# Sigmoid attention and a bilinear feed-forward in one kernel: x in seven blocks of 512 tokens through memory, and twelve float32 pairs

## The chip, the core and the metric

The kernel runs on one NeuronCore of a Trainium2 chip. The metric is the time of one execution in microseconds (us) on the device. A run's profile comes from one execution of its own; its times are not averages.

## The reference

```python
# q, k, v: 8 batches, 12 heads, 448 tokens, 64 wide; float32
scores = q @ k.T / 8 - log(448)
attn   = 1 / (1 + exp(-scores))          # a sigmoid, no row sums
x      = (attn @ v), heads side by side  # 3584 tokens x 768
h      = ((x @ w1) * (x @ w2)) @ w3      # 1024 wide, then 1024 wide
out    = h @ w_out                       # 3584 x 768
```

w1, w2, w3 and w_out come as the words of 64-bit floats, and the kernel makes float32 of them itself.

## The kernel before

**Two kinds of product.** Most products run in a reduced float32 (F32R in the code), with each operand split into a high and a low part: hi x hi, hi x lo and lo x hi are summed, three products in the place of one. `split` makes the two parts: a copy that rounds (ScalarE, VectorE) and a subtraction (VectorE or GpSimd). The alternative is a product in full float32 on unsplit operands. `PLAIN` says how many of the first head pairs do their attention that way; it is 9.

**Stages.** Heads go in pairs: 48 pairs, six to a batch (`pairs`, line 341). A pair has four chunks of keys, taken in the order 0, 3, 1, 2 (line 410); one chunk of one pair is a slot, 192 in all. In a slot TensorE makes the scores of its chunk, ScalarE the sigmoids, and one slot later TensorE multiplies with v (`attend_due`). After the last chunk `combine` (line 260) brings the pair's 128 rows of x into SBUF as two tiles xh and xl of 448 columns, one of the six pieces of 128 rows (kc) that a batch's x has. Two pools, px0 and px1, hold x of even and odd batches.

**Up products.** `up` (line 310) multiplies a batch's x with w1 and w2. For each of eight chunks of 128 features (fc) and each of the two weights (n) it sums 6 pieces x 3 products of 448 columns, so 288 products a batch; then ScalarE copies the first sum and VectorE multiplies the two into g, which is stored in memory (`g_dram`). `up` is a generator: the loop takes 12 products a slot from it (line 435), which stand between a slot's scores and the product with v of the slot before. A batch's products start in slot 2 of the batch behind it (line 432); the last batch's come after attention (line 460), beside the decode of w_out.

**Weights.** A piece of w1 or w2 is a job: load the words (768 KB), take magnitudes on ScalarE (line 79), decode in six VectorE operations (lines 86 to 102), and split three slots later (copy on ScalarE, subtraction on VectorE, line 67). `starts` (line 354) puts eight of the 16 jobs into batch 0, one in three slots, and eight into batch 1, one in 4/3 slots. The 16 pieces of w3 follow from batch 2 on, one in two pairs, loaded two slots ahead of their decode, and are stored in memory at once (line 304).

**Order.** Up to slot 34 (line 417) the order on TensorE, SP, ScalarE and GpSimd is the program's own, and VectorE's is set by a planner; after it, TensorE and SP keep the program's order. All loads and stores are issued on SP, in order. At slot 34 the pool of the weight words (`pp`) closes and the pool of the split attention operands (`pf`) takes its memory. For a split pair VectorE makes qs and kh (lines 158, 159, 66) and GpSimd kl and ks (lines 67, 165), two slots ahead of the pair where the kinds change over.

**Behind.** When the up products are done, w3 x w_out is formed (line 508) and the last product (line 524) goes over all tokens in blocks of 512, with g loaded back from memory.

Of the kernel before, what the change touches and what calls it, by code (L numbers as in the profile page):

```python
# [25 lines left out]
def sigmoid_attention_bilinear_ffn(  # L26
# [42 lines left out]
    def load_words(src, pool=None):  # L69
        if pool is None:  # L70
            raw = pd.tile([P, NK, P, 2], U32, name="raw", bufs=1)[:, :src.shape[1]]
# [5 lines left out]
    def magnitude(raw, early=False):  # L77
        f = (pp if early else pd).tile([P, *raw.shape[1:-1]], F32, name="f", bufs=3 if early else 2)
        nc.scalar.activation(f, raw[..., 1].bitcast(F32), AF.Abs, scale=HW_SCALE)  # L79
        return f  # L80

# [28 lines left out]
    px0 = phase_a.enter_context(tc.tile_pool(name="px0", bufs=NK, side="right"))  # L110
    pa = phase_a.enter_context(tc.tile_pool(name="pa", bufs=2, side="right"))
    px = (px0, px1)
# [69 lines left out]
    def add_halves(dst, src):  # L182

        for j in range(2):
            rows, others = slice(j * D, (j + 1) * D), slice((1 - j) * D, (2 - j) * D)
            nc.scalar.copy(out=dst[rows], in_=src[j][others])  # L186
            nc.vector.tensor_tensor(out=dst[rows], in0=src[j][rows], in1=dst[rows], op=ALU.add)  # L187
# [69 lines left out]
                    start=first and m == 0, stop=last and m == len(ops) - 1,  # L257
                )

    def combine(b, accs):  # L260
        xh = px[b % 2].tile([P, S], F32R, name="xh")
        xl = px[b % 2].tile([P, S], F32R, name="xl")
        if len(accs) == 1:
            split(xh, xl, accs[0][:, :S], nc.scalar.copy, nc.vector)
            return xh, xl
        t = pm.tile([P, S], F32, name="t", bufs=1)
        add_halves(t, [acc[:, :S] for acc in accs])
        split(xh, xl, t, nc.scalar.copy, nc.vector)
        return xh, xl

    wh, wl = {}, {}
    for n in (1, 2):
# [15 lines left out]

    def load_job(i):
        _, _, cs, src = jobs[i]  # L290
        raws[i] = load_words(src[:, cs], pp) if i < EARLY else load_words(src[:, cs])

    def decode_job(i):
        if i + 2 < EARLY:
            load_job(i + 2)
        for k in (i, i + 1):
            if k not in fs and k in raws:
                fs[k] = magnitude(raws[k], k < EARLY)
        f = decode(raws.pop(i), fs[i])
        if EARLY <= i + 1 < len(starts):  # L300
            load_job(i + 1)
# [8 lines left out]
    def up(b, xs, banks):  # L310

        for fc in range(NF):
            for n in (1, 2):
                acc = ps.tile([P, 512], F32, name="up", tag=next(banks), bufs=2)
                for kc in range(NK):
                    xh, xl = xs[kc]
                    for m, (w, x) in enumerate(((wh[n], xh), (wh[n], xl), (wl[n], xh))):
                        nc.tensor.matmul(  # L318
                            acc[:, :S], w[:, fc, kc], x,
                            start=(kc == 0 and m == 0), stop=(kc == NK - 1 and m == 2),  # L320
                        )
                        if (kc, m) != (NK - 1, 2):
                            yield
                if n == 1:
                    a_sb = pm.tile([P, S], F32, name="a_sb", bufs=1)
                    nc.scalar.copy(out=a_sb, in_=acc[:, :S])
                    yield
            g = pm.tile([P, S], F32, name="g", bufs=1)
            nc.vector.tensor_tensor(out=g, in0=acc[:, :S], in1=a_sb, op=ALU.mult)
            nc.sync.dma_start(out=g_dram[fc, :, b * S:(b + 1) * S], in_=g)  # L330
            yield

    def take(stream, n):
        for _ in range(n):
            next(stream, None)
# [6 lines left out]
    zeros = pp.tile([P, 512], F32R, name="zeros", bufs=1)  # L342
    nc.vector.memset(zeros.bitcast(F32), 0.0)

    def idle_products(n):

        acc = ps.tile([P, 512], F32, name="up", bufs=2)
# [5 lines left out]
    first = NPAIR * NC  # L353
    starts = [1 + 3 * i for i in range(8)] + [first + 1 + 4 * i // 3 for i in range(8)]
    assert len(starts) == 2 * NF
    later = [(2 * NPAIR + 2 * i) * NC + 1 for i in range(2 * NF)]
    steps = {}
    for i, s in enumerate(starts):
        steps.setdefault(s + (3 if s < first else 2), []).append((split_job, i))
    for i, s in enumerate(starts + [s + 2 for s in later]):  # L360
        steps.setdefault(s, []).append((decode_job, i))
    for i, s in enumerate(later):
        steps.setdefault(s, []).append((load_job, 2 * NF + i))

    EARLY = sum(s + 2 < PLAIN * NC - 2 for s in starts)
    qks, vvs = {}, {}
    for p in range(2):
        qks[p] = load_pair(*pairs[p])
# [4 lines left out]
    xs = {b: [] for b in range(B)}  # L373
    filler = iter(())
    waiting = []
    accs = {}
# [2 lines left out]
    def attend_due(slot):  # L379
        while waiting and waiting[0][0] <= slot:  # L380
            _, p, c, ops = waiting.pop(0)
            if c == 0:
                accs[p] = [
                    ps.tile([P, 512], F32, name="av", bufs=2) for _ in range(1 if p < PLAIN else 2)
                ]
            attend(c, ops, vs[p], accs[p])
            if c == NC - 2:
                b = pairs[p][0]
                xs[b].append(combine(b, accs.pop(p)))
                del vs[p]  # L390

    def prepare(p, i):
# [84 lines left out]
    TB = 512  # L477
    NH = NF // 2


# [16 lines left out]
    assert NT % TB == 0  # L497
    split_g(0, 0, load_g(0, 0))
    for ic in range(NF):
        w3h, w3l = w3s.pop(ic)  # L500
# [62 lines left out]
```

## Time and profile before

| what | us |
|---|---|
| three timed runs: median, lowest, highest | 1082.26, 1080.23, 1083.45 |
| the profiled execution's own time | 1081.56 |
| its span, first to last instruction | 1079.5 |
| TensorE, VectorE, ScalarE, GpSimd busy in it | 1067.9, 714.1, 563.4, 190.1 |

Busy is the time in which an engine has an instruction of the trace under way. A product's duration in the trace is longer than its share of TensorE, because products overlap; the chain of waits, in which n products in a row stand with the time from the first to the next thing behind them, gives what one takes. PE is TensorE, PEld its weight loads, DVE VectorE, ACT ScalarE, POOL GpSimd, SPq the queue that issues transfers. A line number is the kernel's line; `combine` and `decode` operations carry the helper's line.

### The profile page before, as it was taken

The numbers are of one execution on the slowest core, as the hardware profiler recorded it, in microseconds if no ns is written. First come the engines' busy times: TensorE is split into PE (matmuls) and PEld (weight loads), VectorE is DVE, ScalarE is ACT, GpSimd is POOL, SyncE is SP. The second block draws the span as 40 slices with busy tenths as digits, with TensorE's granted clock in tenths as the row PEclk, the third lists the DMA queues.
The fourth block names the chain that finished last, engine by engine and source line by source line (L and its number), as shares of the span: only waits on it lengthen the run. The fifth ranks groups of instructions, "written<-read, shape, count | busy, mean of one in ns | idle before, by whom it ended". The sixth has DMA issues, their size and how long they took to land.

```text
span 1079.5 us, 14155 instructions
## 1 busy us (share of the span) xinstructions
PE 1067.9 (99%) x5094; PEld 915.1 (85%) x5094; DVE 714.1 (66%) x1074; ACT 563.4 (52%) x789; POOL 190.1 (18%) x277
## 2 busy tenths in 40 slices
PE   8999899999999999999999999999999999999998
PEld 3256799999999999999999989999999888888886
DVE  5997978888878878888887877649862133223321
ACT  5855666776776677767767766653342011101100
POOL 0002432232233323232332224200000000000000
PEclk9999999999999999999999999999999999999999
DMA  8755434443543535344452543225471032233211
GB/s 257 231 166 146 103 95 122 124 132 104 140 118 103 141 107 135 112 131 115 116 154 79 135 122 92 68 75 180 137 243 39 20 127 93 84 127 127 88 49 49
DMA packets 100693, 129.15 MB, mean 120 GB/s; under 512 B 8016, under 2 KB 82960, under 8 KB 100624
## 3 DMA queue, kind: packets, MB, share of 16 engines
q1 hardware_dynamic: 100624, 128.25, 40.6%
q8 instruction: 40, 0.66, 0.3%
q14 instruction: 29, 0.24, 0.1%
HBM read 98.34 MB, written 29.88 MB: 119 GB/s over the span
## 4 chain that ended last, share of the span: by engine, by line
PE 94%; DVE 2%; DMA 1%; ACT 1%; issue 1%; SPq 0%; ACTq 0%
PE up L318 42%; PE up L524 21%; PE av L255 10%; PE sp L199 9%; PE up L508 6%; PE sp L196 2%; PE av L248 2%; PE sp L225 1%; DMA raw<-w 1%; DVE f L102 0%; ACT f L79 0%; DVE w L67 0%; DVE raw L99 0%; DVE f L94 0%; ACT ap L180 0%
## 5 line engine op out<-in xcount | busy, mean ns | idle before, releaser
L318 PE MATMUL up<-xh,w 128*128 128x448 f32 x1536 | 467.2, 368 | 0.0
L318 PEld LDWEIGHTS up<-xh,w 128*128 128x128 f32 x1536 | 288.8, 188 | 31.6 <-issue 5.9
L318 PE MATMUL up<-xl,w 128*128 128x448 f32 x768 | 281.2, 366 | 0.0
L524 PE MATMUL up<-w 128*128 128x512 f32 x1008 | 228.7, 389 | 0.0
L524 PEld LDWEIGHTS up<-w 128*128 128x128 f32 x1008 | 189.2, 188 | 39.2
L180 ACT ACTIVATE ah<-sp,bias 128x896 fp32r<-128x896 f32 x117 | 117.6, 1005 | 114.3 <-PE sp L199 113.5
L217 DVE TENSOR_TENSOR al<-sp,ah 128x896 fp32r<-128x896 f32 x117 | 127.5, 1090 | 50.0 <-ACT sp L180 49.0
L67 POOL TENSOR_TENSOR kl<-kk,kh 128x896 fp32r<-128x896 f32 x39 | 89.5, 2294 | 402.5 <-DVE kh L66 380.3
L318 PEld LDWEIGHTS up<-xl,w 128*128 128x128 f32 x768 | 144.4, 188 | 12.5
L534 DVE COPY o_sb<-up 128x512 f32<-128x512 f32 x42 | 29.0, 691 | 161.0 <-PE up L524 161.0
L66 ACT CAST w<-graw 128x1024 fp32r<-128x1024 f32 x28 | 29.4, 1056 | 175.9 <-PE up L524 170.5
L180 ACT ACTIVATE sp<-sp,bias 128x896 f32<-128x896 f32 x117 | 113.6, 971 | 0.0
L255 PE MATMUL av<-ah,vs 128*128 128x448 f32 x312 | 102.4, 368 | 3.8 <-DVE ah L239 2.7
L255 PE MATMUL av<-al,vs 128*128 128x448 f32 x234 | 86.1, 368 | 0.4 <-DVE al L217 0.4
L199 PE MATMUL sp<-qs,kh 128*128 128x448 f32 x234 | 86.3, 369 | 0.0
L67 POOL TENSOR_TENSOR vs<-vv,vs 128x256 fp32r<-128x256 f32 x78 | 68.2, 885 | 102.8 <-DVE vs L66 95.0
L199 PE MATMUL sp<-qs,kl 128*128 128x448 f32 x234 | 86.3, 369 | 0.0
L239 DVE TENSOR_TENSOR ah<-st,ah 64x448 fp32r<-64x448 f32 x78 | 59.3, 760 | 18.7 <-ACT st L180 16.8
L255 PEld LDWEIGHTS av<-ah,vs 128*128 128x128 f32 x312 | 58.5, 188 | 10.3 <-DVE ah L239 2.8
L79 ACT ACTIVATE f<-raw 128x768 f32<-128x768 f32 (+2 forms) x48 | 34.4, 716 | 48.3 <-DMA raw<-w_out 17.7
L186 ACT COPY t<-av 64x448 f32<-64x448 f32 x78 | 41.3, 529 | 32.3 <-PE av L255 31.2
L180 ACT ACTIVATE ah<-st,bias 64x448 fp32r<-64x448 f32 x78 | 52.2, 670 | 4.0 <-DVE st L187 2.0
(57 smaller groups left out, 1243.4 us busy)
## 6 DMA issues: line engine op xcount, KB each, us to landing
qq<-qT SPq DMA_DIRECT2D x78, 224.0 KB, 3.9
kk<-kT SPq DMA_DIRECT2D x78, 224.0 KB, 4.5
g_dram<-g SPq DMA_DIRECT2D x64, 224.0 KB, 2.0
graw<-g_dram SPq DMA_DIRECT2D x14, 1024.0 KB, 5.3
raw<-w SPq DMA_DIRECT2D x16, 768.0 KB, 5.3
out<-o_sb SPq DMA_DIRECT2D x42, 256.0 KB, 2.0
vv<-vL SPq DMA_DIRECT2D x48, 192.0 KB, 2.8
raw<-w3T SPq DMA_DIRECT2D x16, 512.0 KB, 4.1
```

The source lines that it names most:

```text
L66: hi_engine(out=dst_hi, in_=src)
L67: lo_engine.tensor_tensor(out=dst_lo, in0=src, in1=dst_hi, op=ALU.subtract)
L79: nc.scalar.activation(f, raw[..., 1].bitcast(F32), AF.Abs, scale=HW_SCALE)
L180: nc.scalar.activation(dst, src, AF.Sigmoid, bias=bias[:n], scale=scale)
L186: nc.scalar.copy(out=dst[rows], in_=src[j][others])
L199: nc.tensor.matmul(sp[:, j], k[:, j, at:at + n], qs[:, j], start=m == 0, stop=m == 1)
L217: nc.vector.tensor_tensor(out=al, in0=sp, in1=ah, op=ALU.subtract)
L239: nc.vector.tensor_tensor(out=a[others, j], in0=t[rows], in1=a[rows, j], op=ALU.subtract)
L255: nc.tensor.matmul(accs[j][:, :S], v[:, c, j].rearrange("p u d -> p (u d)"), a[:, j], start=first and m == 0, stop=last and m == len(ops) - 1,
L318: nc.tensor.matmul(acc[:, :S], w[:, fc, kc], x, start=(kc == 0 and m == 0), stop=(kc == NK - 1 and m == 2),)
L508: nc.tensor.matmul(acc[:, :NM], a[:, jc], w[:, jc, ms], start=(jc == 0 and m == 0), stop=(jc == NF - 1 and m == 2),)
L524: nc.tensor.matmul(acc[:, :TB], w[:, fc, ms], g[:, at, fc % NH], start=(fc == 0 and m == 0), stop=(fc == NF - 1 and m == 2),)
```

## The change

x is now kept in seven blocks of 512 tokens (the batches are of 448). The first block stays in SBUF, in six of eight tiles of 2 x 512 columns (high and low part); all of x behind its first 512 tokens is split into `xs`, stored in memory (`x_dram`) two slots later, and loaded by blocks. The up products of block c run in the slots of batches c + 2 and on, from slot 49 for block 0 and from slot 76 for block 1; before slot 76 eleven are taken a slot, then twelve. Each is of 512 columns, and there are 7 x 288 = 2016 of them, 2304 before. Block 6 comes after attention, behind the 48 products that block 5 has left there. Two tiles of the next block are loaded as chunk 6 of the eight feature chunks begins; in chunk 7 the passes of w1 and w2 are interleaved (1: pieces 0 to 3, 2: 0, 1: 4, 2: 1, 1: 5, 2: 2 to 5), and after each of the first four passes of w2 that frees a tile the next tile is asked for. g is stored after the next chunk's first sum has been copied, instead of at once.

Twelve pairs are in full float32, so the kinds change over at slot 46, and all 16 pieces of w1 and w2 are decoded before it, one in 2.7 slots, loaded three jobs ahead. A piece of w3 is loaded in the slot in which its decode stands, and stored five slots later.

```diff
-    PLAIN = 9
+    TB = 512
+    PLAIN = 2 * NPAIR
+    x_dram = dram.tile([NK, P, 2, NT], F32, name="x_dram")
-    px1 = phase_x.enter_context(tc.tile_pool(name="px1", bufs=NK, side="left"))
-    pm = phase_x.enter_context(tc.tile_pool(name="pm", bufs=2, side="left"))
+    px = phase_x.enter_context(tc.tile_pool(name="px", bufs=NK + 2, side="left"))
+    pm = phase_x.enter_context(tc.tile_pool(name="pm", bufs=1, side="left"))
-    pp = phase_p.enter_context(tc.tile_pool(name="pp", bufs=3, side="right"))
+    pp = phase_p.enter_context(tc.tile_pool(name="pp", bufs=4, side="right"))
...
+    def combine(b, kc, accs, due):
         if len(accs) == 1:
+            src = accs[0][:, :S]
+        else:
+            src = pa.tile([P, S], F32, name="t", bufs=1)
+            add_halves(src, [acc[:, :S] for acc in accs])
+        at = b * S
+        n = min(max(TB - at, 0), S)
+        if n:
+            if b == 0:
+                blocks[0][kc] = px.tile([P, 2, TB], F32R, name="x")
+            x = blocks[0][kc][:, :, at:at + n]
+            split(x[:, 0], x[:, 1], src[:, :n], nc.scalar.copy, nc.vector)
+        if n < S:
+            x = pa.tile([P, 2, S], F32R, name="xs")[:, :, n:]
+            split(x[:, 0], x[:, 1], src[:, n:], nc.scalar.copy, nc.vector)
+            stores.append((due, x_dram[kc, :, :, at + n:at + S], x.bitcast(F32), (kc, at + S)))
+
+    def store_due(slot):
+        for entry in [e for e in stores if e[0] <= slot]:
...
+            nc.sync.dma_start(out=entry[1], in_=entry[2])
+
+    def load_block(c, kc):
+        blocks[c][kc] = px.tile([P, 2, TB], F32R, name="x")
+        nc.sync.dma_start(
+            out=blocks[c][kc].bitcast(F32), in_=x_dram[kc, :, :, c * TB:(c + 1) * TB]
+        )
...
     def decode_job(i):
-        if i + 2 < EARLY:
-            load_job(i + 2)
+        if i + 3 < EARLY:
+            load_job(i + 3)
+        elif i >= EARLY:
+            load_job(i)
...
         if n == 3:
-            nc.sync.dma_start(out=w3_dram[at, :, cs], in_=f)
+            stores.append((starts[i] + 5, w3_dram[at, :, cs], f, None))
...
+    def up(c, banks):
+        xs, following = blocks[c], c + 1 if c + 1 in blocks else None
...
         for fc in range(NF):
+            if fc == NF - 2 and following:
+                for kc in range(2):
+                    load_block(following, kc)
+            passes = [(1, kc) for kc in range(NK)] + [(2, kc) for kc in range(NK)]
+            if fc == NF - 1:
+                passes.sort(key=lambda s: s[1] + 3.5 * s[0])
+            accs = {}
+            for n, kc in passes:
+                if kc == 0:
+                    accs[n] = ps.tile([P, TB], F32, name="up", tag=next(banks), bufs=2)
+                for m, (w, i) in enumerate(((wh[n], 0), (wh[n], 1), (wl[n], 0))):
+                    nc.tensor.matmul(
+                        accs[n], w[:, fc, kc], xs[kc][:, i],
+                        start=(kc == 0 and m == 0), stop=(kc == NK - 1 and m == 2),
+                    )
                     yield
+                if (fc, n) == (NF - 1, 2) and following and kc + 2 < NK:
+                    load_block(following, kc + 2)
+                if (n, kc) == (1, NK - 1):
+                    a_sb = pm.tile([P, TB], F32, name="a_sb")
+                    nc.scalar.copy(out=a_sb, in_=accs[1])
+                    if ready:
+                        store(*ready)
+            g = pm.tile([P, TB], F32, name="g")
+            nc.vector.tensor_tensor(out=g, in0=accs[2], in1=a_sb, op=ALU.mult)
+            ready = fc, g
+        store(*ready)
...
-    starts = [1 + 3 * i for i in range(8)] + [first + 1 + 4 * i // 3 for i in range(8)]
-    later = [(2 * NPAIR + 2 * i) * NC + 1 for i in range(2 * NF)]
+    EARLY = 2 * NF
+    starts = [1 + 27 * i // 10 for i in range(EARLY)]
+    starts += [(2 * NPAIR + 2 * i) * NC + 1 for i in range(2 * NF)]
+    steps = {s + 3: [(split_job, i)] for i, s in enumerate(starts[:EARLY])}
     for i, s in enumerate(starts):
         steps.setdefault(s, []).append((decode_job, i))
...
+            store_due(slot)
             prepare(p, i)
...
-            if b > 0 and (hp, i) == (0, 2):
+            if b > 1 and (hp, i) == ((0, 1) if b == 2 else (1, 0)):
                 take(filler, 10 ** 6)
-                filler = up(b - 1, xs[b - 1], itertools.repeat("up"))
-            take(filler, ups)
+                filler = up(b - 2, itertools.repeat("up"))
+            take(filler, ups if slot >= (3 * NPAIR + 1) * NC else ups - 1)
...
     attend_due(slot)
+    store_due(10 ** 6)
     take(filler, 10 ** 6)
...
-    filler = up(B - 1, xs[B - 1], banks)
+    filler = up(NT // TB - 1, banks)
```

## Rows read from the trace of the kernel before

**Rows 1.** The page's busy shares: busy us (share of span) xinstructions of each engine.
```profile
PE 1067.9 (99%) x5094; PEld 915.1 (85%) x5094; DVE 714.1 (66%) x1074; ACT 563.4 (52%) x789; POOL 190.1 (18%) x277
```
**Rows 2.** The page's chain that ended last, share of the span by line.
```profile
PE up L318 42%; PE up L524 21%; PE av L255 10%; PE sp L199 9%; PE up L508 6%; PE sp L196 2%; PE av L248 2%; PE sp L225 1%; DMA raw<-w 1%; DVE f L102 0%; ACT f L79 0%; DVE w L67 0%; DVE raw L99 0%; DVE f L94 0%; ACT ap L180 0%
```
**Rows 3.** Busy us in windows: PE, PEld, DVE, ACT, POOL, clock, DMA share, GB/s.
```profile
0.00:14.00 14.00, 12.23 (x42) 6.21 (x42) 2.61 (x6) 5.19 (x7) 0.20 (x4) 1.00 0.85 259
14.00:58.00 44.00, 42.09 (x182) 10.81 (x184) 43.17 (x60) 36.37 (x45) 0.00 (x0) 1.00 0.77 232
...
157.00:300.00 143.00, 143.00 (x702) 131.42 (x701) 117.73 (x180) 103.33 (x149) 43.47 (x65) 1.00 0.45 120
```
**Rows 4.** The chain of waits in order of time: start us, us, what xcount.
```profile
57.60 0.95 PE sp L196 x4
58.55 2.66 PE up L318 x12
61.21 0.90 PE av L248 x4
...
90.04 1.44 PE up L318 x6
...
122.88 1.49 PE sp L199 x4
...
155.19 0.81 PE sp L199 x4
...
171.54 2.44 PE up L318 x12
...
256.90 2.46 PE up L318 x12
...
714.79 2.02 PE av L255 x10
716.81 63.30 PE up L318 x312
780.12 67.08 PE up L508 x384
847.19 228.54 PE up L524 x1008
```
**Rows 5.** Timeline of VectorE in batch 0: start us, us, engine, line, operation.
```profile
20.40 0.95 DVE L67 TENSOR_TENSOR w<-f,w 128x768 fp32r<-128x768 f32 x1
...
32.20 0.95 DVE L67 TENSOR_TENSOR w<-f,w 128x768 fp32r<-128x768 f32 x1
...
36.61 0.62 DVE L67 TENSOR_TENSOR xl<-av,xh 128x448 fp32r<-128x448 f32 x1
37.14 0.95 DVE L102 TENSOR_TENSOR f<-f,raw 128x768 f32<-128x768 f32 x1
38.01 0.95 DVE L67 TENSOR_TENSOR w<-f,w 128x768 fp32r<-128x768 f32 x1
```
**Rows 6.** Groups by line: operation xcount, busy us, mean ns, idle before and releaser.
```profile
L159 DVE TENSOR_TENSOR qs<-qq,qs 64x896 fp32r<-64x896 f32 x39 | 44.7, 1146 | 1.3
...
L158 DVE CAST qs<-qq 128x896 fp32r<-128x896 f32 x39 | 24.5, 629 | 12.6 <-DMA qq<-qT 12.4
L66 DVE CAST kh<-kk 128x896 fp32r<-128x896 f32 x39 | 24.3, 622 | 0.4
...
L67 POOL TENSOR_TENSOR kl<-kk,kh 128x896 fp32r<-128x896 f32 x39 | 89.5, 2294 | 402.5 <-DVE kh L66 380.3 <-PE up L318 14.9 <-PE sp L199 7.3
```
**Rows 7.** Transfers by issuing line: xcount, KB each, median us to landing.
```profile
graw<-g_dram SPq DMA_DIRECT2D x14, 1024.0 KB, 5.3
...
raw<-w3T SPq DMA_DIRECT2D x16, 512.0 KB, 4.1
```
**Rows 8.** Who waited for whom: us in total, times, longest us.
```profile
ACT f L79 <- DMA raw<-w3T: 5.4, 5, 2.7
...
PE av L255 <- DVE t L187: 1.0, 1, 1.0
```

More of the change, by code (lines that the diff above doesn't have):

```diff
@@ L55, in sigmoid_attention_bilinear_ffn @@
     scale = 1.0 / math.sqrt(D)
-    PLAIN = 9
+    TB = 512
+    assert NT % TB == 0 and S <= TB <= 2 * S
+    PLAIN = 2 * NPAIR
     pw = ctx.enter_context(tc.tile_pool(name="pw", bufs=4))
@@ L67, in split, with load_words @@
         lo_engine.tensor_tensor(out=dst_lo, in0=src, in1=dst_hi, op=ALU.subtract)
-    def load_words(src, pool=None):
-        if pool is None:
-            raw = pd.tile([P, NK, P, 2], U32, name="raw", bufs=1)[:, :src.shape[1]]
+    def load_words(src, pool):
+        if pool is pd:
+            raw = pd.tile([P, NF // 2, P, 2], U32, name="raw", bufs=1)
         else:
@@ L75, in load_words, with magnitude @@
         return raw
-    def magnitude(raw, early=False):
-        f = (pp if early else pd).tile([P, *raw.shape[1:-1]], F32, name="f", bufs=3 if early else 2)
+    def magnitude(raw, pool=pd):
+        f = pool.tile([P, *raw.shape[1:-1]], F32, name="f", bufs=3 if pool is not pd else 2)
         nc.scalar.activation(f, raw[..., 1].bitcast(F32), AF.Abs, scale=HW_SCALE)
@@ L106, in sigmoid_attention_bilinear_ffn @@
     phase_x = ExitStack()
-    px1 = phase_x.enter_context(tc.tile_pool(name="px1", bufs=NK, side="left"))
-    pm = phase_x.enter_context(tc.tile_pool(name="pm", bufs=2, side="left"))
+    px = phase_x.enter_context(tc.tile_pool(name="px", bufs=NK + 2, side="left"))
+    pm = phase_x.enter_context(tc.tile_pool(name="pm", bufs=1, side="left"))
     phase_a = ExitStack()
-    px0 = phase_a.enter_context(tc.tile_pool(name="px0", bufs=NK, side="right"))
     pa = phase_a.enter_context(tc.tile_pool(name="pa", bufs=2, side="right"))
-    px = (px0, px1)
     phase_p = ExitStack()
-    pp = phase_p.enter_context(tc.tile_pool(name="pp", bufs=3, side="right"))
+    pp = phase_p.enter_context(tc.tile_pool(name="pp", bufs=4, side="right"))
     bias = pm.tile([P, 1], F32, name="bias", bufs=1)
@@ L258, in attend @@
                 )
-    def combine(b, accs):
-        xh = px[b % 2].tile([P, S], F32R, name="xh")
-        xl = px[b % 2].tile([P, S], F32R, name="xl")
+    blocks = {c: {} for c in range(NT // TB)}
+    stores, stored = [], {}
+    def combine(b, kc, accs, due):
         if len(accs) == 1:
[L264 to L269, printed above, removed]
+            src = accs[0][:, :S]
[15 more added lines that the diff above has]
+        for entry in [e for e in stores if e[0] <= slot]:
+            stores.remove(entry)
+            if entry[3]:
+                kc, end = entry[3]
+                stored[kc] = end
+            nc.sync.dma_start(out=entry[1], in_=entry[2])
+    def load_block(c, kc):
+        assert stored[kc] >= (c + 1) * TB
+        blocks[c][kc] = px.tile([P, 2, TB], F32R, name="x")
+        nc.sync.dma_start(
+            out=blocks[c][kc].bitcast(F32), in_=x_dram[kc, :, :, c * TB:(c + 1) * TB]
+        )
     wh, wl = {}, {}
@@ L290, in load_job @@
         _, _, cs, src = jobs[i]
-        raws[i] = load_words(src[:, cs], pp) if i < EARLY else load_words(src[:, cs])
+        raws[i] = load_words(src[:, cs], pp if i < EARLY else pd)
     def decode_job(i):
-        if i + 2 < EARLY:
-            load_job(i + 2)
+        if i + 3 < EARLY:
+            load_job(i + 3)
+        elif i >= EARLY:
+            load_job(i)
         for k in (i, i + 1):
-            if k not in fs and k in raws:
-                fs[k] = magnitude(raws[k], k < EARLY)
+            if k in raws and k not in fs:
+                fs[k] = magnitude(raws[k], pp if k < EARLY else pd)
         f = decode(raws.pop(i), fs[i])
-        if EARLY <= i + 1 < len(starts):
-            load_job(i + 1)
         n, at, cs, _ = jobs[i]
         if n == 3:
-            nc.sync.dma_start(out=w3_dram[at, :, cs], in_=f)
+            stores.append((starts[i] + 5, w3_dram[at, :, cs], f, None))
     def split_job(i):
@@ L308, in split_job, with store @@
         split(wh[n][:, at, cs], wl[n][:, at, cs], fs.pop(i), nc.scalar.copy, nc.vector)
-    def up(b, xs, banks):
-        for fc in range(NF):
[L313 to L326, printed above, removed]
-                    yield
[L328 to L331, printed above, removed]
+    def up(c, banks):
+        xs, following = blocks[c], c + 1 if c + 1 in blocks else None
+        ready = None
+        def store(fc, g):
+            nc.sync.dma_start(out=g_dram[fc, :, c * TB:(c + 1) * TB], in_=g)
+        for fc in range(NF):
+            if fc == NF - 2 and following:
[13 more added lines that the diff above has]
+                    )
+                    yield
+                if (fc, n) == (NF - 1, 2) and following and kc + 2 < NK:
[9 more added lines that the diff above has]
+        store(*ready)
@@ L341, in sigmoid_attention_bilinear_ffn @@
     pairs = [(b, hp) for b in range(B) for hp in range(NPAIR)]
-    zeros = pp.tile([P, 512], F32R, name="zeros", bufs=1)
+    zeros = pp.tile([P, TB], F32R, name="zeros", bufs=1)
     nc.vector.memset(zeros.bitcast(F32), 0.0)
     def idle_products(n):
-        acc = ps.tile([P, 512], F32, name="up", bufs=2)
+        acc = ps.tile([P, TB], F32, name="up", bufs=2)
         for _ in range(n):
@@ L351, in sigmoid_attention_bilinear_ffn @@
     idle_products(12)
-    first = NPAIR * NC
-    starts = [1 + 3 * i for i in range(8)] + [first + 1 + 4 * i // 3 for i in range(8)]
-    assert len(starts) == 2 * NF
-    later = [(2 * NPAIR + 2 * i) * NC + 1 for i in range(2 * NF)]
-    steps = {}
+    EARLY = 2 * NF
+    starts = [1 + 27 * i // 10 for i in range(EARLY)]
+    starts += [(2 * NPAIR + 2 * i) * NC + 1 for i in range(2 * NF)]
+    steps = {s + 3: [(split_job, i)] for i, s in enumerate(starts[:EARLY])}
     for i, s in enumerate(starts):
-        steps.setdefault(s + (3 if s < first else 2), []).append((split_job, i))
-    for i, s in enumerate(starts + [s + 2 for s in later]):
         steps.setdefault(s, []).append((decode_job, i))
-    for i, s in enumerate(later):
-        steps.setdefault(s, []).append((load_job, 2 * NF + i))
-    EARLY = sum(s + 2 < PLAIN * NC - 2 for s in starts)
+    assert starts[EARLY - 1] + 3 < PLAIN * NC - 2
     qks, vvs = {}, {}
@@ L372, in sigmoid_attention_bilinear_ffn @@
     splits, vs = {0: split_pair(0 < PLAIN, *qks.pop(0))}, {0: split_v(0 < PLAIN, vvs.pop(0))}
-    xs = {b: [] for b in range(B)}
+    load_job(2)
     filler = iter(())
@@ L387, in attend_due @@
             if c == NC - 2:
-                b = pairs[p][0]
-                xs[b].append(combine(b, accs.pop(p)))
+                combine(*pairs[p], accs.pop(p), slot + 2)
                 del vs[p]
@@ L475, in sigmoid_attention_bilinear_ffn @@
     p4 = ctx.enter_context(tc.tile_pool(name="p4", bufs=2, side="left"))
-    TB = 512
     NH = NF // 2
@@ L495, in split_g @@
             split(ghs[:, at, fs], gls[:, at, fs], g[:, fs], nc.scalar.copy, nc.vector)
-    assert NT % TB == 0
     split_g(0, 0, load_g(0, 0))
```

## The prediction

> **What bounds the kernel now.** I read the page's busy shares first: TensorE is busy for 99% of the span [rows 1]. A busy TensorE need not be a full one, so the chain of waits comes next: 42% of it is the up products of line 318, 21% the last product of line 524, 10% the attention products of line 255 [rows 2]. TensorE thus sets the end, and the question is what each product costs and where the engine is held up. The windows show where other engines come near: between 14 and 58 us, batch 0, VectorE is busy 43.17 of 44 us and DMA moves 232 GB/s at a share of 0.77; between 157 and 300 us the share is 0.45 [rows 3]. The chain in order of time gives the prices [rows 4]. A chunk of a float32 pair (a slot: scores 0.95, attention times v 0.90) takes 1.85 us of TensorE. Twelve up products of 448 columns take 2.44 us where x lies in one pool and 2.46 in the other, 203.3 and 205.0 ns each, and 2.66 us between float32 products. After attention 312 take 63.30 us, 202.9 each. The last product's 512 columns take 228.54/1008 = 226.7 ns, the 384 columns of line 508 67.08/384 = 174.7. The four products at 155.19 open slot 48 (pair 12); the up products end at 780.12, and the rest of the span, 299.4 us, is not touched.
>
> **The change, part by part.** I split the span at slot 48, since in the new kernel everything before it is float32 attention without up products, and everything behind it is what the old kernel does there, with 2016 up products of 512 columns instead of the 2040 of 448 that it still has at that point (2304 less the 264 of slots 26 to 47).
>
> *Behind slot 48.* The old kernel takes 780.12 - 155.19 = 624.9 us. Of that 1728 products at 204.2 and 312 at 202.9 are 352.9 + 63.3 = 416.2 us; the other 208.7 us are 36 pairs of attention and one wait of 1.0 us [rows 8], which I count below, so 207.7. In place of the 416.2 stand 2016 x 226.7 = 457.0 us, and the stretch grows to 664.7 us. The price of a 512-column product on x is not in the trace. From above it is 233.4 ns (the loop's 204.2 x 512/448: no gain by width), from below 225.4 (226.7 less the 1.3 by which places differ). I take 226.7: it is measured, on the same width and the same kind of operands. The Trainium skill (TensorE: Matmul & The Clock Gate, section Back-to-back issue gap) has a warm product cost N/2.4 + 2.5 ns, a fixed part too small for widening to pay: 2304 x 189.2 against 2016 x 215.8, 0.9 us in all. The rows differ from it at both widths, by 14 and by 11 ns, so I go by them; that width brings nothing is a rival below.
>
> *Before slot 48.* The old kernel needs 155.19 us, with 264 up products and three split pairs in it, and with a jam where the pairs change over: from 90.04 to 122.88 it gets through the rest of a float32 slot (2.66 + 0.90), two whole ones (1.85 + 2.66 each) and one split pair (15.5, a quarter of the stretch's mean of four slots: 559.6/36), 28.1 us, so 4.7 go there. The new kernel has 48 float32 slots. On TensorE alone slot 48 would come 22 x 1.85 = 40.7 us after slot 26, which begins at 57.60: at 98.3. But all 16 weight pieces of w1 and w2 are now decoded in those slots, one each 2.7 slots = 5.0 us, and VectorE needs more. Its row of the split of line 67 recurs after 5.81 us (32.20 to 38.01) with a combine of 0.53 in between, so a piece is 5.3 us [rows 5]. At 20.40 two pieces are decoded. Fourteen more are 74.2 us; eleven combines 5.8; the second part that a combine of batch 1 has (448 cut into 64 and 384) about 0.15 x 5 = 0.7. So the last decode ends at 101.1, and two splits of 0.95 end at 103.0. Only then is the memory of the weight pieces free for pair 12, whose qs and kh take 2.4 us on VectorE (0.63 + 1.15 + 0.62) and whose kl takes 2.3 on GpSimd [rows 6]: 107.7. VectorE, not TensorE, sets this stage, and the 4.7 us of the jam are not lost again, since no decode stands between these operations. Bounds: 98.3 if VectorE keeps up, 112.4 if a jam like the old one comes back. I take 107.7, from the nearest rows.
>
> Sum: 107.7 + 664.7 = 772.4 for the end of the up products against 780.1, 7.7 us less, before waits.
>
> *x through memory.* 42 stores (one a pair from the seventh on) and 36 loads are new. SP's issues hide beside TensorE, and so do the stores: x of a pair is needed only much later, except the last pair's, which has the 48 up products left after attention. What can show is the change of blocks. Six x tiles of a block and two spare ones: two tiles of the next block are loaded a chunk ahead, the others as the last chunk frees them. That chunk has twelve passes of three products; the sixth tile is asked for after the tenth pass and used in the eighteenth (the next block's sixth). Seven passes of 0.68 us lie between, 1 3/4 slots or 7.3 us inside attention (a slot is 3.9 us now, 12 x 22.5 ns more then), 4.8 us after it. A load of 512 KB lands in 4.1 us (w3 words), one of 1024 KB in 5.3 [rows 7]: alone, in time. But from the fifth pass to the eighteenth, about 12.6 us, the queue carries four loads (2.1 MB), q and k of a pair (four of 64 x 2 x 448 float32, 0.9 MB), a store of x (0.46) and one of g (0.26), 3.7 MB or 295 GB/s, and 232 GB/s at a share of 0.77 means 301 when full [rows 3]. So each of six changes lies between no wait and some 3 us (at the 259 GB/s of the first 14 us the same bytes take 1.7 us more, and landing itself varies by the 1.2 between the two rows). I take 0.4 us each, 2.5 in all, because the tiles come in the order of use and q and k have slack of slots. Queued behind a waiting product on TensorE is all else, so a wait counts in full. Behind a waiting load on SP stand the next loads of q, k and v, due slots later.
>
> *w3 pieces.* Words and decode now stand in one slot; before, the load came two slots ahead. ScalarE's abs waits for them: five of 16 waited in the old kernel, 5.4 us, 2.7 at most, and TensorE lost 1.0 once [rows 8]. Next slots have 0.27 us more of TensorE work each as cover. From below nothing, from above 16 x 1.0; I take 0.6. The late stores of g and w3 free SP, on which TensorE does not wait: nothing. g's buffer is single and its store now leaves half a chunk later, with 18 products (6 us) before its next use; if a store lands late VectorE waits: in the same allowance. Copies and products of g are 56 instead of 64, off the path.
>
> Total: -7.7 + 2.5 + 0.6 = -4.6 against the profiled execution's 1081.56 (span 1079.5 and 2.1 around it), which lies 0.7 under the median of the runs: **1077.0**.
>
> **Rivals.** *Late tiles (slower side).* At each change of blocks the last two tiles land after their pass. For: the queue's 295 GB/s against 301, and the change after attention has only 4.8 us and the w_out words beside it. Against: the share around is 0.45, and q and k wait for GpSimd, so bursts need not coincide. Price 3 us x 6 = 18: 1081.6 - 7.7 + 0.6 + 18 = 1092; the gain is gone from 1.2 us each.
> *Width brings nothing.* A 512-column product costs 233.4: 2016 x 6.7 = 13.5 us more, 1090. For: the two 448-column pools already differ. Against: line 524's 1008 products at 226.7. The gain is gone from 226.7 + 4.6/2.016 = 229.0.
> *ScalarE stands at the w3 words.* Each of 16 loads costs TensorE 1.0 us: 15.4 more than taken, 1092. For: load and use stand together. Against: eleven of 16 did not wait, and of five waits one reached TensorE.
> *TensorE sets the front.* VectorE's backlog drains under the slots: slot 48 near 99.5, 8 us less, 1069. For: batch 0's chain runs on TensorE for most of 21 to 58 us. Against: VectorE's 43.17 of 44 us at three slots a piece.
>
> **How the numbers follow.** Forecast with its small waits (1073 to 1081) 0.52; TensorE's front 0.10; late tiles, from 1 us each up to the full price, 0.18; width 0.07; w3 words 0.13. A measurement tells 0.3%, 3.2 us, from no change: below 1079.0 is faster, above 1085.5 slower. Faster: three quarters of the forecast's 0.52, all of 0.10 and 0.06 of the rest, where the waits or the width take only part of their price: 0.55. Slower: half of the three cases with waits or no width, 0.19. The rest, 0.26, is the same. Range 1068 to 1088: TensorE's front below, half of each slow rival's price above; the forecast's own is 1073 to 1081.
>
> **What would show it.** Right: up products at 226.7 ns, twelve in 2.72 us; VectorE without gaps from 14 to 103 us and slot 48's scores near 107; TensorE's waits on x loads six, under half a microsecond each. Wrong: up products above 229; the scores of slot 48 after 112; TensorE idle before up products until DMA into x for over 1 us a change; ScalarE's abs waiting over 15 us in all for the w3 words with TensorE idle behind it. The prediction fails as a whole if the sum of such waits passes 7.7 us, or slot 48 comes before 100.

## The result and the profile after

The changed kernel takes **1088.43 us** (median of six, 1086.97 to 1089.11) against 1081.8 of the kernel before: ratio 1.0062, 95% interval 1.0048 to 1.0075. The forecast was 1077.0: wrong in sign. The profiled execution takes 1087.51 us, its span 1085.7.

The page's busy shares, then the chain by line (the row in which the forecast looked for the gain):

```profile
PE 1065.1 (98%) x4818; PEld 850.3 (78%) x4818; DVE 686.2 (63%) x1030; ACT 545.9 (50%) x760; POOL 170.6 (16%) x256
...
PE up L358 40%; PE up L559 21%; PE av L256 9%; PE sp L200 8%; PE up L543 6%; PE sp L226 1%; PE av L249 1%; PE sp L197 1%; DVE w L70 1%; DVE f L97 1%; DMA raw<-w 1%; DMA qp<-kT 1%; DVE raw L102 1%; DVE f L105 1%; DMA x<-x_dram 1%
```

The up products' share fell from the 42% of [rows 2], but VectorE's lines and DMA now stand in the chain at 1% each: TensorE no longer runs through from the first slot to the last. The windows say where (us, PE, PEld, DVE, ACT, POOL busy, granted clock, DMA share, GB/s):

```profile
14.00:58.00 44.00, 39.20 (x170) 9.92 (x168) 43.28 (x62) 35.08 (x43) 0.00 (x0) 1.00 0.80 249
58.00:100.00 42.00, 35.95 (x150) 9.06 (x152) 41.24 (x61) 31.17 (x42) 0.00 (x0) 0.96 0.55 176
100.00:112.00 12.00, 10.97 (x48) 3.11 (x48) 6.62 (x9) 7.28 (x10) 4.92 (x7) 1.00 0.73 191
112.00:145.00 33.00, 30.36 (x134) 24.53 (x133) 28.31 (x38) 20.82 (x31) 9.97 (x15) 1.00 0.64 160
157.00:300.00 143.00, 142.19 (x645) 120.53 (x644) 115.01 (x172) 98.02 (x141) 42.73 (x63) 1.00 0.58 167
```

From 14 to 100 us VectorE is nearly full and TensorE lacks 11 us; between 100 and 112 neither is full; from 112 to 145, where the kinds of pair change over, TensorE lacks 2.6. From 157 on it is all but full (142.19 of 143), as in [rows 3]. The chain in order of time, inside attention and behind it:

```profile
251.96 2.75 PE up L358 x12
254.71 1.24 PE av L256 x6
255.94 0.83 PE sp L200 x4
256.77 2.75 PE up L358 x12
...
710.07 8.88 PE up L358 x39
...
724.93 61.95 PE up L358 x272
786.88 3.12 PE up L543 x18
```

Twelve products take 2.75 us where 2.72 was forecast: 229.2 ns each, and 227.8 in the row of 272 (61.95/272). The first five behind attention's 448 columns take 232.5, 235.9, 228.3, 232.5 and 230.9 from start to start, most of the rest 226.7.

Stage by stage, from the first score product of a slot. In the changed kernel those of slots 48 and 56 are these (start us, us, line, operation; in brackets the idle time before it and its releaser):

```profile
110.25 0.44 PE L200 MATMUL sp<-qs,kh 128*128 128x448 f32 x1 [0.27 <-DVE qs L160]
...
143.65 0.37 PE L200 MATMUL sp<-qs,kh 128*128 128x448 f32 x1
```

| | before | forecast | after |
|---|---|---|---|
| slot 48 begins | 155.0 | 107.7 | 110.2 |
| slot 56 begins | 186.1 | | 143.6 |
| up products end | 780.1 | 775.5 | 786.9 |
| the rest of the span | 299.4 | 299.4 | 298.8 |

The 11.4 us between forecast and trace come out as: front +2.5; slots 48 to 56 +4.4 (33.4 us, where 56 attention products at 0.207 and 77 up products at 0.227 need 29.0; I go on calling this loss the jam); up products +4.1 (0.028 at each of 143 changes of width); attention +1.1 (a pair's period, 16.77, less 48 products leaves 5.77 us, before 15.54 leaves 5.74); one loss of 1.0 at 220 us (slot 75 has only the last two up products of block 0, where its neighbours have eleven, so TensorE comes early to attention times v and stands for 0.81 us until VectorE has made `al`, the low part of the sigmoids); x tiles -1.2 (1.3 where 2.5 was forecast); w3 words -0.6. Sum 11.3.

### The profile page after: what moved, and what is told of

It reads as the page before. It is cut to its first block, busy times and chain, and to the rows that moved or that the text cites. A ratio compares the mean times of both kernels' runs of the same rounds, so it can differ in the third digit from the quotient of the medians.

```text
span 1085.7 us, 13615 instructions
## 1 busy us (share of the span) xinstructions
PE 1065.1 (98%) x4818; PEld 850.3 (78%) x4818; DVE 686.2 (63%) x1030; ACT 545.9 (50%) x760; POOL 170.6 (16%) x256
## 4 chain that ended last, share of the span: by engine, by line
PE 88%; DVE 6%; DMA 3%; ACT 1%; issue 1%; SPq 1%; POOL 0%; DVEq 0%; ACTq 0%
PE up L358 40%; PE up L559 21%; PE av L256 9%; PE sp L200 8%; PE up L543 6%; PE sp L226 1%; PE av L249 1%; PE sp L197 1%; DVE w L70 1%; DVE f L97 1%; DMA raw<-w 1%; DMA qp<-kT 1%; DVE raw L102 1%; DVE f L105 1%; DMA x<-x_dram 1%
## 5 line engine op out<-in xcount | busy, mean ns | idle before, releaser
L358 PE MATMUL up<-x,w 128*128 128x512 f32 x2016 | 485.7, 391 | 0.1
L358 PEld LDWEIGHTS up<-x,w 128*128 128x128 f32 x2016 | 378.1, 188 | 78.0 <-DMA x<-x_dram 2.0
L181 ACT ACTIVATE ah<-sp,bias 128x896 fp32r<-128x896 f32 x108 | 108.7, 1006 | 133.8 <-PE sp L200 133.7
L218 DVE TENSOR_TENSOR al<-sp,ah 128x896 fp32r<-128x896 f32 x108 | 117.9, 1091 | 78.5 <-ACT sp L181 76.7
L70 POOL TENSOR_TENSOR kl<-kk,kh 128x896 fp32r<-128x896 f32 x36 | 76.8, 2134 | 361.4 <-DVE kh L69 221.4
L181 ACT ACTIVATE sp<-sp,bias 128x896 f32<-128x896 f32 x108 | 104.9, 971 | 0.0
L256 PE MATMUL av<-ah,vs 128*128 128x448 f32 x288 | 94.9, 369 | 2.4 <-DVE ah L240 1.5
L240 DVE TENSOR_TENSOR ah<-st,ah 64x448 fp32r<-64x448 f32 x72 | 47.8, 664 | 22.7 <-ACT st L181 21.1
L249 PE MATMUL av<-ap,vv 128*64 128x448 f32 (+1 forms) x192 | 47.4, 572 | 11.6 <-ACT ap L181 11.4
L181 ACT ACTIVATE ap<-sp,bias 128x896 f32<-128x896 f32 (+1 forms) x48 | 47.5, 1005 | 15.7 <-PE sp L197 15.7
```

What stands on the lines that cost most here:

```text
L181: nc.scalar.activation(dst, src, AF.Sigmoid, bias=bias[:n], scale=scale)
L218: nc.vector.tensor_tensor(out=al, in0=sp, in1=ah, op=ALU.subtract)
L240: nc.vector.tensor_tensor(out=a[others, j], in0=t[rows], in1=a[rows, j], op=ALU.subtract)
L249: nc.tensor.matmul(accs[0][cols, :S], v[:ops[0].shape[0], c, cols], ops[0][:, j], start=first, stop=last,)
L256: nc.tensor.matmul(accs[j][:, :S], v[:, c, j].rearrange("p u d -> p (u d)"), a[:, j], start=first and m == 0, stop=last and m == len(ops) - 1,
L358: nc.tensor.matmul(accs[n], w[:, fc, kc], xs[kc][:, i], start=(kc == 0 and m == 0), stop=(kc == NK - 1 and m == 2),)
```

## The experiments

Times and ratios are against the kernel before on the same chip.

**Is it the traffic of x?** Stores and loads of x are left out and all blocks use the first block's tiles, so later blocks' values are not computed.

```diff
-            stores.append((due, x_dram[kc, :, :, at + n:at + S], x.bitcast(F32), (kc, at + S)))
...
-        blocks[c][kc] = px.tile([P, 2, TB], F32R, name="x")
...
+        blocks[c][kc] = blocks[c - 1][kc]
```

> The changed kernel without the stores and loads of x: all seven blocks use the first block's tiles, so the later blocks' values are left out. Theory (the loss is on VectorE and on TensorE's own prices): only the waits on x loads go, 1.3 us, and some crowding of the q, k and v loads; 1085 to 1087.5 against 1088.4, and the jam of the first split pairs (slot 48 to 56 in 33.4 us) stays over 32. Rival (x's 36 MB of traffic makes q, k, v late and so makes the jam): 1083 or less, and slots 48 to 56 in under 31 us.

Measured: 1092.03, ratio 1.0087 (1.0073 to 1.0101). From 157 to 300 us the DMA share falls from 0.58 to 0.42, yet slot 48 stays at 110.7, slots 48 to 56 at 34.1 us and an up product at 229.1: x's transfers make neither the front nor the jam nor the price. The total rises, above both forecasts, and can't be set against the changed kernel's, since the edit also moved VectorE's order: in 35 of 36 split pairs the copy kh now runs before the subtraction of qs (in the changed kernel in one of 36), and so GpSimd's kl beside that subtraction. GpSimd is busy for 51.66 instead of 42.73 us of the window; its kl there, in the changed kernel and in this run (count, busy us, mean ns):

```profile
L70 POOL TENSOR_TENSOR kl<-kk,kh 128x896 fp32r<-128x896 f32 x9 | 19.1, 2128 | 61.0 <-DVE kh L69 42.9 <-PE av L256 18.1
...
L70 POOL TENSOR_TENSOR kl<-kk,kh 128x896 fp32r<-128x896 f32 x9 | 25.0, 2777 | 43.7 <-DVE kh L69 39.7 <-issue 4.0
```

VectorE's subtraction of qs goes from 1.18 to 1.43 us. TensorE waits for VectorE at some pairs (`al` 2.1 us, `t`, the sum of a pair's halves, 1.4); that the new order makes these waits was not tested.

**Is the front held by loads that come late?** Words asked for two jobs ahead instead of three, so that q and k don't queue behind them.

```diff
-        if i + 3 < EARLY:
-            load_job(i + 3)
+        if i + 2 < EARLY:
+            load_job(i + 2)
...
-    load_job(2)
```

> Weight words asked for two jobs ahead, as before, with the four word buffers kept: SP then never stands at a word load that waits for a buffer. Theory (in the front, q and k of the next pair are late because SP stands at a word load): TensorE's waits of 3.7 us at 39, 56 and 85 us go, slot 44 with the last split comes some 3 us earlier, slot 48 at 106 to 107.5 instead of 110.2; 1084.5 to 1086. Rival (VectorE alone sets the front): no change, 1088.

Measured: 1088.33, 1.0057 (1.0045 to 1.0070). TensorE's waits in the front fall from 11.4 to 8.6 us, the longest from 3.7 to 2.0, and slot 48 stays at 110.2. My theory fell, the rival held. One thing runs the other way: windows of 1 us have TensorE's granted clock at 0.50 from 37 to 43 and from 75 to 77 us, in the changed kernel only from 76 to 78. But VectorE ends its last split but one at 100.6 us in both, and the last split waits for slot 44 in both.

**Is it the order of the last jobs?** The changed kernel's VectorE around the last split (start us, us, line, operation; in brackets the idle time before it and its releaser):

```profile
98.75 0.95 DVE L105 TENSOR_TENSOR f<-f,raw 128x768 f32<-128x768 f32 x1
99.66 0.96 DVE L70 TENSOR_TENSOR w<-f,w 128x768 fp32r<-128x768 f32 x1
104.61 0.96 DVE L70 TENSOR_TENSOR w<-f,w 128x768 fp32r<-128x768 f32 x1 [3.98 <-ACT w L69]
...
105.61 0.62 DVE L159 CAST qs<-qq 128x896 fp32r<-128x896 f32 x1
106.23 0.63 DVE L69 CAST kh<-kk 128x896 fp32r<-128x896 f32 x1
...
107.36 2.75 DVE L160 TENSOR_TENSOR qs<-qq,qs 64x896 fp32r<-64x896 f32 x1
```

VectorE has caught up at 100.6, then stands for 3.98 us, because ScalarE's copy for job 15 belongs to slot 44 and TensorE is only there. One slot earlier:

```diff
-    starts = [1 + 27 * i // 10 for i in range(EARLY)]
+    starts = [1 + 13 * i // 5 for i in range(EARLY)]
```

> Pieces of w1 and w2 every 2.6 slots instead of 2.7, so the last job stands one slot earlier (decode in slot 40, split in 43). Theory A (in the changed kernel VectorE had caught up at 100.6 us and then stood idle for 3.98 us, because ScalarE's copy for the last split belongs to slot 44): the copy comes one float32 slot of 1.85 us earlier, slot 48 opens at 108.0 to 109.0 instead of 110.2, total 1086.0 to 1087.5. Theory B (VectorE alone sets the front, by the sum of its work): the same work stands in it, slot 48 within 0.5 us of 110.2, total 1088 to 1089.

Measured: 1089.97, 1.0079 (1.0065 to 1.0092); slot 48 at 112.9, against both theories. VectorE stands for 4.15 us before the last split here too, and slot 43, in which the copy now stands, begins at 102.7 us instead of 99.9: TensorE itself is late. The windows of 5 us show what neither had (columns as above):

```profile
60.00:65.00 5.00, 2.96 (x16) 0.82 (x16) 4.90 (x8) 3.50 (x6) 0.00 (x0) 1.00 0.66 201
65.00:70.00 5.00, 5.00 (x14) 0.93 (x10) 4.86 (x8) 2.29 (x4) 0.00 (x0) 0.50 0.66 189
...
80.00:85.00 5.00, 3.19 (x16) 0.85 (x16) 4.93 (x9) 3.74 (x7) 0.00 (x0) 1.00 0.77 252
85.00:90.00 5.00, 5.00 (x18) 1.19 (x16) 4.90 (x8) 2.97 (x4) 0.00 (x0) 0.66 0.50 169
```

With the jobs closer together TensorE does not stand longer in all (its waits for the sigmoids between 14 and 112 us are 10.0 us, in the changed kernel 11.4), but after three of its waits, of 1.88 us at 46, 2.04 at 65 and 1.81 at 85 us, its granted clock falls to the lower level (0.50, 1.2 GHz) for some microseconds. The changed kernel has one such fall (the chain of it, start us, us, what):

```profile
72.54 1.01 ACT ap L181
73.60 0.97 PE av L249 x4
74.57 1.22 PE sp L197 x4
75.78 1.69 PE av L249 x4
77.48 1.49 PE sp L197 x4
78.97 0.90 PE av L249 x4
```

After a wait of 3.7 us for the sigmoids three groups take 4.40 us instead of 2.80. A wait for VectorE's pace can thus cost TensorE a second time. Why the clock falls after some waits and not after others was not tested.

**Is it VectorE's work?** Three of the six decode operations are left out for w1 and w2: what the low words add is not computed.

```diff
+        if not low_too:
+            return f
         nc.vector.tensor_scalar(out=high, in0=fb, scalar1=0xFF800000, scalar2=None, op0=ALU.bitwise_and)
...
-        f = decode(raws.pop(i), fs[i])
+        f = decode(raws.pop(i), fs[i], i >= EARLY)
```

> Of the decode of w1 and w2 the last three of six VectorE operations are left out (0.56 + 0.96 + 0.96 us a piece, 39 us in all); this leaves out what the low words of the 64-bit floats add to these two weights. Theory A (VectorE's work sets the front of the changed kernel, and ScalarE and TensorE only hand its pace on): slot 48 opens at 98 to 101 instead of 110.2, TensorE's waits on ScalarE's sigmoids in the front fall from 8 us to under 1, its granted clock stays at 1.00, and the total is 1077 to 1080. Theory B (the front is held by the arrival of the words and by loads behind them on SP, or by TensorE's lower clock whatever VectorE does): slot 48 at 105 to 110, total 1083 to 1088.

Measured: 1077.09, 0.9952 (0.9938 to 0.9966), slot 48 at 99.2. Its windows of the front, and what TensorE waited for between 14 and 112 us (us, times, longest), which in the changed kernel is 11.4, 9, 3.7 for the same line:

```profile
14.00:58.00 44.00, 43.64 (x192) 11.31 (x192) 29.19 (x43) 39.40 (x49) 0.00 (x0) 1.00 0.88 270
58.00:100.00 42.00, 39.38 (x172) 10.29 (x168) 25.79 (x40) 32.78 (x44) 3.94 (x6) 1.00 0.65 200
```

```profile
PE av L251 <- ACT ap L183: 2.8, 4, 0.8
```

The clock stays at 1.00 and slot 48 comes 0.9 us behind TensorE's own 98.3. So VectorE's work sets the front, and ScalarE, which copies and takes magnitudes in the program's order between the sigmoids, hands its pace on: between 14 and 112 us it waits 12.7 us for VectorE's x and `w` tiles in the changed kernel, 3.9 here. All 11 us reach the total; slots 48 to 56 still take 33.4.

**Can GpSimd take some of it?** The subtraction of the split of w1 and w2:

```diff
-        split(wh[n][:, at, cs], wl[n][:, at, cs], fs.pop(i), nc.scalar.copy, nc.vector)
+        split(wh[n][:, at, cs], wl[n][:, at, cs], fs.pop(i), nc.scalar.copy, nc.gpsimd)
```

> The changed kernel with the subtraction of the w1 and w2 splits on GpSimd, which is idle in the front, instead of VectorE. Theory (VectorE's 5.3 us a weight piece sets the front): 0.9 us a piece goes from VectorE, 14 us in all, TensorE's 1.85 us a slot takes over, slot 48 at 99 to 103 instead of 110.2 us, 1079 to 1083. Rival (GpSimd's work slows VectorE as much, or ScalarE's order sets the front): slot 48 at 109 or later, 1087 or more.

Measured: 1102.14, 1.0186 (1.0172 to 1.0200), slot 48 at 120.2. The rival held. The timeline of the two engines:

```profile
60.08 1.81 POOL L70 TENSOR_TENSOR w<-f,w 128x768 fp32r<-128x768 f32 x1 [4.36 <-ACT w L69]
60.11 2.60 DVE L97 SCALAR_TENSOR_TENSOR f<-f,raw 128x768 uint32<-128x768 uint32 x1
62.73 0.56 DVE L101 TENSOR_SCALAR raw<-f 128x768 uint32<-128x768 uint32 x1
...
66.67 0.98 DVE L97 SCALAR_TENSOR_TENSOR f<-f,raw 128x768 uint32<-128x768 uint32 x1
67.11 2.20 POOL L70 TENSOR_TENSOR w<-f,w 128x768 fp32r<-128x768 f32 x1 [5.22 <-ACT w L69]
67.68 2.06 DVE L101 TENSOR_SCALAR raw<-f 128x768 uint32<-128x768 uint32 x1
```

The operation that meets GpSimd's takes 2.60 instead of 0.98, or 2.06 instead of 0.56: VectorE stands while GpSimd works, and where they meet 0.95 us saved cost 1.5 to 1.6. The Trainium skill (SBUF — State Buffer, section SBUF: two separate sides) says that the two engines share one pair of ports as an exclusive lock, which GpSimd's operation, or one of VectorE's with two inputs in SBUF or in a two-port mode, holds for a whole instruction. Both rows agree: VectorE's operation ends 0.8 and 0.4 us behind GpSimd's, with 0.98 and 0.56 of its own. The qs row of 2.75 us above meets GpSimd's first kl (107.08 to 109.15) in the same way; [rows 6] has 1.15 on the mean.

**Is the jam of slots 48 to 56 made of w3's decode and of the buffers of q and k?** First each alone (three pairs later; a fourth buffer), then both, with two pairs.

```diff
-    starts += [(2 * NPAIR + 2 * i) * NC + 1 for i in range(2 * NF)]
+    starts += [(2 * NPAIR + 3 + 2 * i) * NC + 1 for i in range(2 * NF)]
```

> The w3 pieces start three pairs later (pair 15 instead of pair 12), so that no decode falls to the first split pairs. Theory (VectorE is overfull in slots 48 to 56, 3.5 us of it w3 decode): slots 48 to 56 take 30 to 31 us instead of 33.4, 1085 to 1086.5. Rival (the jam comes from the q and k loads of pair 13, which wait for a free buffer): 33 us, 1088.

Measured: 1087.93, 1.0053 (1.0040 to 1.0066). Slots 48 to 56 take 31.3 us instead of 33.4, but slots 76 to 80 give 3.7 back, where a piece of w3 now meets the first change of blocks and up products wait 1.9 us for x.

```diff
-        qq = pa.tile([P, 2, S], F32, name="qq", tag="qk", bufs=3)
...
+        qq = pa.tile([P, 2, S], F32, name="qq", tag="qk", bufs=4)
...
```

> A fourth buffer for q and k, so that pair 13's loads need not wait for the split of pair 12. Theory (VectorE's work makes the jam): at most 1 us less, 1087.4 to 1088.4. Rival (late q and k make it): slots 48 to 56 in about 30 us, 1084.5 to 1086.

Measured: 1088.12, 1.0062 (1.0048 to 1.0075). Slots 48 to 56 take 32.3 us, 1.1 less, most of it given back later. In the changed kernel SP stood as long at the load of q for pair 13 (us, times, longest):

```profile
SPq L136 <- POOL kl L70: 1.1, 1, 1.1
```

Both:

```diff
-    starts += [(2 * NPAIR + 2 * i) * NC + 1 for i in range(2 * NF)]
+    starts += [(2 * NPAIR + 2 + 2 * i) * NC + 1 for i in range(2 * NF)]
...
-        qq = pa.tile([P, 2, S], F32, name="qq", tag="qk", bufs=3)
...
+        qq = pa.tile([P, 2, S], F32, name="qq", tag="qk", bufs=4)
...
```

> Fourth buffer for q and k, and each w3 piece two pairs later (so none stands in the pair in which the kinds change over). Theory A (the jam of slots 48 to 56 is made of a wait for the q/k buffer and of w3's decode in the same slots): slots 48 to 56 take 30 us or less instead of 33.4, the end of the up products comes 3 us earlier, total 1085 to 1086. Theory B (the jam is GpSimd's and VectorE's backlog of operand splits, which these two don't touch): 31.5 us or more, and the later slots give it back, total 1087.5 to 1088.5.

Measured: 1085.32, 1.0033 (1.0020 to 1.0045), 3.1 us below the changed kernel. Slots 48 to 56 take 30.2 us. The window from 110 to 143 us, in the changed kernel:

```profile
110.00:143.00 33.00, 30.11 (x131) 23.61 (x131) 26.95 (x39) 21.17 (x31) 11.97 (x20) 1.00 0.61 155
```

and with both edits:

```profile
110.00:143.00 33.00, 32.67 (x146) 26.54 (x146) 25.73 (x37) 22.21 (x32) 12.82 (x21) 1.00 0.65 165
```

TensorE gets 2.6 us back, with less work of VectorE in the window and a little more of GpSimd's. These two make three quarters of the jam.

**Is the price of an up product one of width or of change?** Twice the products in every second slot halves the changes.

```diff
-            take(filler, ups if slot >= (3 * NPAIR + 1) * NC else ups - 1)
+            late = slot >= (3 * NPAIR + 1) * NC
+            if slot % 2 == late:
+                take(filler, 2 * (ups if late else ups - 1))
```

> Up products taken 24 in every second slot instead of 12 in each: half as many changes from attention products to up products. Theory (each change costs 28 ns, in the first five up products behind it): mean price in the loop 228.0 ns instead of 229.2, 2 us less on TensorE, total 1085.5 to 1088 since other engines now get uneven slots. Rival (the price belongs to the stage, that is to other engines' traffic, or to the place of x): 229.2 stays.

Its chain:

```profile
301.75 5.47 PE up L358 x24
307.21 0.83 PE av L256 x4
308.04 1.65 PE sp L200 x8
309.69 5.47 PE up L358 x24
```

24 take 5.47, so the second twelve take 2.72, the forecast's figure; the loop's mean falls from 229.2 to 227.9 ns. The 0.028 us belong to the change. The total is 1095.7, 1.0126 (1.0110 to 1.0141), where the forecast had 1085.5 to 1088: in slots of unequal length TensorE waits longer for VectorE and GpSimd (`al` 2.8, `t` 2.7, `ks` 1.3 us). From slot 48 on these waits are 4 us more than in the changed kernel; the rest was not traced.

And the changed structure with eight blocks of 448 columns, all 2304 products; the last two blocks now come after attention:

```diff
-    TB = 512
...
+    TB = S
...
-    filler = up(NT // TB - 1, banks)
+    filler = itertools.chain(up(NT // TB - 2, banks), up(NT // TB - 1, banks))
...
```

> The changed kernel with blocks of 448 tokens, eight of them, all else as changed (the last product keeps its 512). Theory (width is worth what the rows say): 2304 products at 204.5 in the loop and 202.9 behind it, 470.2 us, instead of 461.2: 9 us more, 1096 to 1099. Rival (width brings nothing): 1087 to 1090.

```profile
302.99 2.44 PE up L358 x12
305.43 0.82 PE sp L200 x4
```

Twelve take 2.44, with no price of change: 203.3 ns each. 2304 x 203.3 = 468.4 us against 461.6 (1680 x 229.2 in the loop and 336 x 227.8 behind it), so width does pay, 6.8 us in all where the forecast had 2304 x 204 less 2016 x 226.7 = 13.0. The rule that the Trainium skill (TensorE: Matmul & The Clock Gate, section Back-to-back issue gap) gives for an isolated warm product gave 0.9 as an estimate; the section says that this rule counts too much for wide products in a stream, and here it counts too little (215.8 ns against 226.7). What width is worth lies between the two. The total is 1104.17, 1.0208 (1.0194 to 1.0222), above both forecasts: the up products end at 802.2, with a tail of 624 products at 213.4, in which stand four of the five waits for tiles of x (4.2 of 4.4 us).

**What do float32 pairs cost by themselves?** The kernel before with twelve:

```diff
-    PLAIN = 9
+    PLAIN = 12
```

> The kernel before with 12 float32 pairs instead of 9 and nothing else. Theory (a float32 pair costs TensorE 1.7 us more than a split one, and up products between float32 products 0.22 us a slot): 5.1 + 2.6 us more, the jam of 4.7 us at the change of kinds may shrink; 1085 to 1090. Rival (float32 pairs relieve VectorE and pay for themselves): 1082 or less.

Measured: 1083.05, 1.0013 (1.0005 to 1.0022), between the two forecasts; slot 48 at 156.4, 1.4 later than with nine. With ten:

```diff
-    PLAIN = 9
+    PLAIN = 10
```

> The kernel before with 10 float32 pairs in place of 9 (nothing else changed; all 16 pieces of w1 and w2 are then decoded before the kinds change over). Theory A (the jam of the old kernel at the changeover, 4.7 us, comes of decodes that stand between the first operand splits; twelve pairs removed it and cost 6 us in slower attention): one more pair costs 2 us, the jam goes at least by half: 1079 to 1081.5. Theory B (the jam comes of the changeover itself): 1083 to 1084.5.

Measured: **1078.95, 0.9974 (0.9964 to 0.9983)**; slot 48 at 152.1. From ten pairs to twelve it comes 4.3 us later, so a pair costs 2.15, and the tenth takes away a jam of 155.0 + 2.15 - 152.1 = 5.0 us. The 4.7 that the forecast read there were right. With a fourth buffer for q and k as well:

> The kernel before with 10 float32 pairs and a fourth buffer for q and k. Theory A (part of the jam is the wait for a q/k buffer that GpSimd's kl still reads): 0.5 to 1.5 us below the kernel with 10 pairs alone. Theory B (loads of q and k arrive in time in the old kernel): within 0.4 us of it.

Measured: **1078.13, 0.9963 (0.9951 to 0.9976)**, 0.8 below ten pairs alone, the intervals overlapping. Its attention ends at 712.9 (before 716.8). This is the fastest full kernel here, 3.8 us below the one before and 10.3 below the changed one.

## Why the prediction was wrong

**The step that failed first: "the 4.7 us of the jam are not lost again, since no decode stands between these operations."** 4.4 us are lost. The old jam was made of w1's and w2's decodes between the first operand splits; those are gone. But w3's first decode stands in the first split pair, in slot 49, and the load of q for pair 13 waits until GpSimd's kl frees a buffer. Moving one and adding the other brings 3.2 of the 4.4 back there, 3.1 in the total. I looked at what was removed from between these operations and not at what the `starts` list puts there.

**The price of an up product, "it is measured, on the same width and the same kind of operands."** Right for products in a row, mis-sized in a loop that changes between 448 and 512 columns 143 times: 229.2 instead of 226.7, 4.1 us in all. The row that it rested on is an unbroken run. I had called the gain gone from 229.0, by another cause, with a chance of 0.07.

**VectorE sets the front: right, mis-sized.** 110.2 instead of 107.7. The decodes ended at 99.7, sooner than my 101.1, but "two splits of 0.95 end at 103.0" took the last split as ready: it waits for a copy in slot 44, on a TensorE that had itself lost time to sigmoids and to the lower clock, and ended at 105.6. That the stage costs far more than TensorE's own time was in the forecast (9.4 us over 98.3; it came to 11.9); that TensorE's clock falls in it, and three times with closer jobs, was not.

**x through memory: right.** TensorE's waits for x in all, from the page's line of weight loads:

```profile
L358 PEld LDWEIGHTS up<-x,w 128*128 128x128 f32 x2016 | 378.1, 188 | 78.0 <-DMA x<-x_dram 2.0
```

2.0 us on the weight loads, of which some 1.3 reached the products, where I took 2.5, although the tiles land later than [rows 7] made me think (transfers by issuing line: xcount, KB, median us to landing):

```profile
x<-x_dram SPq DMA_DIRECT2D x36, 512.0 KB, 6.6
...
x_dram<-xs SPq DMA_DIRECT2D x36, 448.0 KB, 3.4
g_dram<-g SPq DMA_DIRECT2D x56, 256.0 KB, 3.4
...
raw<-w3T SPq DMA_DIRECT2D x16, 512.0 KB, 4.9
```

The lead of 7.3 us held, but for pauses of some 0.1 us a tile. ScalarE never waits for w3's words: the 0.6 was nothing.

**The rivals.** Late tiles and ScalarE's words are refuted, TensorE's front too; that width brings nothing is refuted by the run with 448 columns, though a total near its 1090 came about, by other causes. The true rival, a new jam where the old one was, stood only as a bound of the front (112.4), not as a case with a chance.

**What stays open.** About 1.2 us of the jam; attention's 0.03 us a pair; how much of its time the run without transfers of x lost to VectorE's new order; why TensorE's clock falls after some of its waits and not after others.

## What to carry to other kernels

When a stage is emptied of one kind of work, list what the new schedule puts into it before booking the old stall as gained: here the wait was rebuilt from other work in the same slots. Take the price of an instruction from a row with the same neighbours, not only the same shape. And give each part of a change a run of its own: one more float32 pair, with the old blocks, made the kernel 3 us faster, while the whole change made it 6.6 us slower.

## What the hardware showed that was not expected

- A product of 512 columns behind ones of 448 costs 0.028 us more in all, spread over its first five; 448 behind 448 does not (203.3 ns each in the loop).
- VectorE operations that began behind one of GpSimd's took 2.06 to 2.75 us instead of 0.56 to 1.15, one with one input among them. It is not so for all: `al`, one of whose two inputs lies in PSUM, took 1.09 us beside GpSimd's work as without it.
- After TensorE had stood for 3.7 us, the groups of float32 products behind it took 1.22 to 1.69 us instead of 0.90 to 0.95, with a granted clock of 0.50 from 76 to 78 us.
